# Reordering the projection prepass of a two-branch attention kernel, and the weight loads around it

## The chip, the cores and the metric

The kernel runs on one core of one Trainium2 chip. The metric is the device time of one execution in microseconds (us), taken as the median of several runs. Lower is better.

## The reference, cut to what matters

Two attention branches over the same 2048 tokens of 640 features are mixed by a gate.

```python
def _A_ref(x, mem0, Wq, Wk, Wv, Wo, seg_len):      # H=32 heads of Dh=192, M=8 memory rows, seg_len=32
    mem = mem0
    for s in range(n_seg):                           # 64 segments, one after the other
        h = concat([mem, x[:, s*32:(s+1)*32]], axis=1)      # 40 rows
        q, k, v = h @ Wq, h @ Wk, h @ Wv             # 640 -> 32 heads x 192, each
        p = softmax(where(mask, q k^T * scale, -1e9))
        o = (p v) @ Wo
        mem = o[:, :8]                               # carried to the next segment
        outs.append(o[:, 8:])

def _B_ref(x, wqkv, wo):   # 32 heads of 20; each query sees 8 keys at distance 0, 2, ..., 14
    ...

g = sigmoid((x * gate_w).sum(-1, keepdims=True))
return g * _A_ref(...) + (1 - g) * _B_ref(x, B_wqkv, B_wo)
```

Branch A is a recurrence: segment s+1 needs the first eight output rows of segment s.

## The kernel before, in words

**Order of the work.** The program runs four stages. `part_b` computes branch B and stores its gated result (`bsc_dram`), and on the way it stores the transposed inputs that branch A needs: `xh_dram` (one block of 40 columns a segment) and `zT_dram` (of each segment the last eight rows, 512 columns in all). `prepass` computes ahead of the recurrence the Q, K and V projections of those 512 columns, and stores them by segment in `zpk_dram`. `part_a` is the recurrence of 64 segments. `part_z` at its end makes the output rows that the recurrence leaves out.

**The weights of branch A.** Wq, Wk, Wv and Wo are cut into 80 slices of 128 partitions x 1536 bf16 (384 KB each, 3 KB of a partition): `("q", R, kc)`, `("k", R, kc)` and `("v", R, kc)` for four groups of heads R and five blocks kc of 128 input features, twelve `("oa", i)` and eight `("ob", i)` of Wo. Fourteen (`stream_keys`, N_STREAM) don't stay in SBUF: they are loaded again for every use into the five buffers of `wstream` (tile `wst`). The other 66 stay. Before, eleven of these are loaded early, in part B (`load_early`, tiles `wres_...`; q slices), and 55 late (tiles `wlate_...`) in three parts: 33 after part B into the room that it leaves, 21 after the Q/K projections of the prepass, and one after the prepass. The slices of Wo that are streamed (three) are first copied, early, from DRAM to a scratch tensor in DRAM (`wscr`), in which each partition's 3 KB lie in one piece; in `A_Wo` itself they are pieces of 768 or 512 bytes.

**The prepass.** `zT` holds the 512 columns, and `zTi` the same ordered by row within the segment (copied by GpSimd). First q, then k, each in two rounds `Rp` of two groups R: 24 outputs of 128 x 512 a round, five matmuls each (L424), which ACT and DVE in turn (`evac`, L71 and L73) copy from PSUM into a staging tile `ZS` (24 KB of a partition, two buffers). A round ends with one store of 3 MB on ACT's queue (L429), in pieces of 384 bytes. Then come the four V rounds: each has four tiles of 128 columns, three PSUM banks a tile (L438), copied into `ZV` (3 KB, two buffers), and each tile is stored by two DMAs of 192 KB on ACT's queue (L445), in pieces of 768 bytes. PSUM has eight banks, used in turn as `ps_pre`.

**Queues.** All weight loads are issued on SP's queue (`nc.sync`). On the same queue are, in part B, the stores of `xh_dram` (L182) and `zT_dram` (L187), from single-buffered tiles that GpSimd fills, and the loads of the gate. ACT's queue (`nc.scalar`) has the loads of x, the stores of `bsc_dram`, the load of `zT`, all stores of the prepass and all small loads of the recurrence (`hT`, `ZQ`, the last columns of `hT` from the initial memory in `A_mem`). An engine issues in its program order, so a DMA that has to wait holds up what stands behind it on that engine. Outside the recurrence the order of each engine's instructions, and the semaphores, are made by the builder from the data dependences, its own estimates of time and the order of the text; `tc.issue_after(first_store)` keeps the early loads and the prepass behind the first store of part B. In the recurrence PE, ACT and DVE follow an order written by hand. SBUF is full to within a few KB of a partition: pools that are closed make room for later ones, and a tile in such a place waits for what lay there (`reuse_waits="tile"`: tile by tile).

Of the kernel before, what the change touches and what calls it, by code (L numbers as in the profile page):

```python
# [10 lines left out]
BF = mybir.dt.bfloat16  # L11
F32 = mybir.dt.float32
I32 = mybir.dt.int32

N_STREAM = 14
N_LATE = 55
N_LATE2 = 22
WBUFS = 5

_DEV = {"mode": "full"}  # L20
# [4 lines left out]
class _K:  # L25
# [313 lines left out]
    def weights_setup(self):  # L339
        nc, tc = self.nc, self.tc  # L340
        keys = self.slice_keys()
        gap = {("q", 0, 0): 300, ("k", 0, 1): 160, ("k", 0, 3): 70, ("k", 1, 0): 450, ("k", 2, 0): 850, ("k", 3, 0): 1050,
               ("v", 1, 0): 1000, ("v", 2, 0): 600, ("v", 3, 0): 570, ("v", 3, 3): 200, ("oa", 6): 1200}
        at, t = {}, 0
        for k in keys:
            t += gap.get(k, 0)
            at[k] = t
            t += 163
        self.stream_keys = set()
        for i in range(N_STREAM):  # L350
            left = [k for k in keys if k not in self.stream_keys]
            self.stream_keys.add(min(left, key=lambda k: abs(at[k] - (i + 0.5) * t / N_STREAM)))
        rest = [k for k in keys if k not in self.stream_keys]
        first = ["q", "k", "v", "oa", "ob"]
        self.late = sorted(rest, key=lambda k: first.index(k[0]))[-N_LATE:]
        self.wres = self.ctx.enter_context(tc.tile_pool(name="wres", bufs=1))
        self.res_tiles = {}
        self.wscr = {}
        self.early = [k for k in rest if k not in self.late]
        self.wstream = self.ctx.enter_context(tc.tile_pool(name="wstream", bufs=WBUFS))  # L360

    def load_early(self):

        for k in self.early:
            self.res_tiles[k] = self.load_slice(self.wres, k, "wres_" + "_".join(map(str, k)))
        so = sorted(k for k in self.stream_keys if k[0] in ("oa", "ob"))
        scr = self.dram.tile([len(so), 128, 1536], BF, name="wscr")
        for i, k in enumerate(so):
            src, split = self.slice_info(k)
            self.nc.sync.dma_start(scr[i].rearrange("p (c f) -> p c f", c=split[0]), src)  # L370
            self.wscr[k] = scr[i]
# [10 lines left out]
            self.nc.sync.dma_start(v[:], src)  # L382
        return v

    def load_late(self, part):

        pool = self.ctx.enter_context(self.tc.tile_pool(name=f"wlate{part}", bufs=1, reuse_waits="tile"))
        ks = (self.late[:-N_LATE2], self.late[-N_LATE2:-1], self.late[-1:])[part]
        first = ks[:4] if part == 1 else []
        place = [k for k in ks if k not in first] + first  # L390
        tiles = {k: pool.tile([128, 1536], BF, name="wlate_" + "_".join(map(str, k))) for k in place}
        for k in ks:
            self.res_tiles[k] = self.load_slice(None, k, None, t=tiles[k])

    def get_slice(self, key):
        if key in self.res_tiles:
            return self.res_tiles[key]
        return self.load_slice(self.wstream, key, "wst", "wst")

    def prepass(self):  # L400

        nc, tc, KC = self.nc, self.tc, self.KC
        nseg = self.S // self.seg
        NZ = nseg * 8
        self.zpk_dram = self.dram.tile([nseg, 128, 1152], BF, name="zpk_dram")
        with tc.tile_pool(name="pre_zv", bufs=2, side="right", reuse_waits="tile") as zvp:
            zTi = zvp.tile([128, KC, NZ], BF, name="zTi", bufs=1)
            with tc.tile_pool(name="pre_zs", bufs=2, reuse_waits="tile") as zp, \
                    tc.tile_pool(name="pre_zt", bufs=1, reuse_waits="tile") as ztp:
                zT = ztp.tile([128, KC, NZ], BF, name="zT")  # L410
                nc.scalar.dma_start(zT[:], self.zT_dram[:].rearrange("p c s i -> p c (s i)"))
                nc.gpsimd.tensor_copy(zTi[:].rearrange("p c (i s) -> p c i s", i=8),
                                      zT[:].rearrange("p c (s i) -> p c i s", i=8))
                for m in ("q", "k"):
                    for Rp in range(2):
                        ZS = zp.tile([128, nseg, 192], BF, name="ZS")
                        for r in range(2):
                            sls = [self.get_slice((m, 2 * Rp + r, kc)) for kc in range(KC)]
                            for j in range(4):
                                for t in range(3):  # L420
                                    ps = self.pst([128, NZ], F32, name="ps_pre")
                                    c0 = 384 * j + 128 * t
                                    for kc in range(KC):
                                        nc.tensor.matmul(ps[:], lhsT=sls[kc][:, c0:c0 + 128], rhs=zT[:, kc, :],  # L424
                                                         start=(kc == 0), stop=(kc == KC - 1))
                                    zc = 96 * r + 8 * (4 * t + j)
                                    self.evac(ZS[:, :, zc:zc + 8], ps[:].rearrange("p (s i) -> p s i", i=8))
                        z0 = 768 + 192 * (1 - Rp) if m == "q" else 384 + 192 * Rp
                        nc.scalar.dma_start(self.zpk_dram[:, :, z0:z0 + 192].rearrange("s p f -> p s f"), ZS[:])  # L429
            self.load_late(1)  # L430
            for R in range(4):
                sls = [self.get_slice(("v", R, kc)) for kc in range(KC)]
                for st in range(NZ // 128):
                    ZV = zvp.tile([128, 1536], BF, name="ZV")
                    pss = [self.pst([128, 512], F32, name="ps_pre") for _ in range(3)]
                    for kc in range(KC):
                        for g in range(3):
                            nc.tensor.matmul(pss[g][:], lhsT=zTi[:, kc, 128 * st:128 * st + 128],  # L438
                                             rhs=sls[kc][:, 512 * g:512 * g + 512], start=(kc == 0),
                                             stop=(kc == KC - 1))  # L440
                    for g in range(3):
                        self.evac(ZV[:, 512 * g:512 * g + 512], pss[g][:])
                    for k in range(2 * st, 2 * st + 2):
                        dst = self.zpk_dram[:, 8 * R + k:128:32, 0:384]
                        nc.scalar.dma_start(dst, ZV[64 * (k % 2):64 * (k % 2) + 64, :].rearrange(  # L445
                            "s (j f) -> s j f", j=4))

    def build_sel(self, pool, ones):
        nc = self.nc
# [469 lines left out]
```

## Time and profile before

| | |
|---|---|
| three timed runs | 1772.72, 1776.31 and 1780.4 us; median 1776.31 |
| span of the profiled execution | 1775.1 us (the page has no other time of this execution) |
| PE busy | 1674.0 us (94%) |
| ACT, DVE, POOL busy | 870.1 (49%), 651.2 (37%), 72.7 us (4%) |
| DMA | 461.12 MB, mean 260 GB/s; SP's queue 395.75 MB, ACT's 60.12 MB |
| granted TensorE clock, mean | 0.991 |

The stages, read off the timeline: part B to 225.6 us; the prepass's Q and K to 332.0, its V to 397.4; the recurrence from 408.1 to about 1712, some 20.4 us a segment; then `part_z`. PE is busy when a matmul is in its pipeline, so 94% is not 94% of its peak. A line number is that of the code above; L71 and L73 are `evac`'s, L382 the load in `load_slice`, L370 the copy to scratch.

### The profile page before, as it was taken

Reading aid. Unit: us, or ns where it says so; the run is one execution under the profiler, and the core shown is the slowest. Engines: PE = TensorE matmul, PEld = TensorE weight load, DVE = VectorE, ACT = ScalarE, POOL = GpSimd, SP = SyncE. Lnnn points to the kernel's source line nnn. Section 1 sums busy time; section 2 is a strip of 40 time slices with the busy share of each in tenths; the row PEclk is TensorE's granted clock in tenths of the full one; section 3 lists DMA queues with packets and bytes.
Section 4 is the critical chain, followed back from the end, with each engine's and each line's share of the span. In section 5 each row is a group of like instructions: output and inputs, shape, how many; then the busy total and the mean of one; then the engine's idle time right before and its main releaser. Section 6 shows DMA issues by size and latency. Waiting matters only on the chain.

```text
span 1775.1 us, 82404 instructions
## 1 busy us (share of the span) xinstructions
PE 1674.0 (94%) x36512; PEld 997.3 (56%) x36527; DVE 651.2 (37%) x2047; ACT 870.1 (49%) x2377; POOL 72.7 (4%) x151
## 2 busy tenths in 40 slices
PE   6998999887999999999999999999999999999989
PEld 3554644334565655555556555555555556555557
DVE  4556533222333333333333333333333333333320
ACT  3766622223555555555555555555545555545550
POOL 4001000002000000000000000000000000000000
PEclk9999999998999999999999999999999999999999
DMA  6610195798899999999999999999999999989981
GB/s 164 203 32 29 46 315 171 207 283 233 293 301 307 305 300 301 300 299 304 300 294 304 308 293 308 298 297 297 305 292 299 301 297 304 303 289 300 299 282 30
DMA packets 280968, 461.12 MB, mean 260 GB/s; under 512 B 97188, under 2 KB 158116, under 8 KB 280612
## 3 DMA queue, kind: packets, MB, share of 16 engines
q1 hardware_dynamic: 173464, 395.75, 67.5%
q10 hardware_dynamic: 107148, 60.12, 11.9%
q8 instruction: 285, 4.67, 1.0%
q14 instruction: 71, 0.58, 0.1%
HBM read 421.44 MB, written 35.52 MB: 257 GB/s over the span
## 4 chain that ended last, share of the span: by engine, by line
PE 84%; ACT 6%; DMA 4%; issue 3%; DVE 2%; ACTq 1%; DVEq 0%
PE ps_qk L540 25%; PE ps_v L633 13%; PE ps_wo L697 11%; PE ps_qkT L557 6%; PE ps_pre L424 6%; PE ps_S L587 5%; PE ps_oT L656 3%; PE ps_z L851 3%; PE ps_bqk L220 3%; ACT bP L243 2%; DMA zpk_dram<-ZV 2%; ACT ZQ L778 2%; PE ps_mem L707 1%; PE ps_S L596 1%; PE ps_bv L207 1%
## 5 line engine op out<-in xcount | busy, mean ns | idle before, releaser
L549 ACT CAST KV<-ps_qk 128x384 bf16<-128x384 f32 x448 | 208.7, 480 | 340.2 <-PE ps_qk L540 196.5
L540 PEld LDWEIGHTS <-hT 128*32 128x32 bf16 x10240 | 247.7, 96 | 163.8 <-issue 21.0
L540 PE MATMUL ps_qk<-wlate_k,hT 128*32 128x384 bf16 x4352 | 270.0, 329 | 2.0 <-issue 2.0
L564 DVE COPY ZQ<-ps_qkT 128x384 bf16<-128x384 bf16 x256 | 91.6, 358 | 382.4 <-PE ps_qkT L557 216.8
L633 PE MATMUL ps_v<-wlate_v,hT 128*32 128x384 bf16 x4096 | 225.3, 330 | 0.0
L605 ACT ACTIVATE ZQ<-ps_S 32x224 bf16<-32x224 f32 x512 | 178.1, 348 | 43.7 <-PE ps_S L596 38.2
L697 PEld LDWEIGHTS <-KV 128*32 128x32 bf16 x6144 | 154.3, 96 | 67.0 <-issue 19.1
L540 PE MATMUL ps_qk<-wres_q,hT 128*32 128x384 bf16 x2816 | 164.2, 330 | 11.9 <-DMA hT<-in_A_mem_dram 10.7
L540 PE MATMUL ps_qk<-wst,hT 128*32 128x384 bf16 x1792 | 154.1, 328 | 0.6 <-DMA hT<-in_A_mem_dram 0.3
L633 PEld LDWEIGHTS <-hT 128*32 128x32 bf16 x5120 | 113.6, 96 | 66.8 <-issue 4.4
L697 PE MATMUL ps_wo<-wlate_oa,KV 128*32 128x384 bf16 x2560 | 140.4, 327 | 2.0 <-DVE ZQ L676 1.0
L587 PE MATMUL ps_S<-ZQ,KV 128*128 128x160 bf16 (+1 forms) x1024 | 136.9, 238 | 0.7 <-DMA ZQ<-zpk_dram 0.7
L697 PE MATMUL ps_wo<-wlate_ob,KV 128*32 128x256 bf16 x2688 | 124.2, 275 | 7.6 <-issue 7.5
L557 PE MATMUL ps_qkT<-ident,KV 128*128 128x128 bf16 x1536 | 130.0, 220 | 0.4 <-issue 0.4
L557 PEld LDWEIGHTS <-KV 128*128 128x128 bf16 x1536 | 89.0, 98 | 61.0 <-issue 40.8
L667 DVE CAST KV<-ps_oT 128x192 bf16<-128x192 f32 x256 | 79.2, 351 | 62.7 <-PE ps_oT L661 62.7
L587 PEld LDWEIGHTS <-KV 128*128 128x128 bf16 (+1 forms) x1024 | 58.8, 95 | 69.5 <-issue 42.2
L667 ACT CAST KV<-ps_oT 128x192 bf16<-128x192 f32 x256 | 69.6, 326 | 57.3 <-PE ps_oT L661 57.3
L710 DVE CAST hT<-ps_mem 128x24 bf16<-128x24 f32 x126 | 22.5, 179 | 199.1 <-PE ps_mem L707 199.1
L640 ACT CAST KV<-ps_v 128x384 bf16<-128x384 f32 x192 | 92.4, 481 | 3.3 <-PE ps_v L633 0.2
L633 PE MATMUL ps_v<-wst,hT 128*32 128x384 bf16 x1024 | 87.1, 330 | 2.4 <-DMA wst<-in_A_Wv_dram 2.4
L568 DVE COPY KV<-ps_qkT 128x384 bf16<-128x384 bf16 x256 | 89.0, 348 | 0.6 <-PE ps_qkT L557 0.4
(135 smaller groups left out, 2262.7 us busy)
## 6 DMA issues: line engine op xcount, KB each, us to landing
wst<-in_A_Wq_dram SPq DMA_DIRECT2D x260, 384.0 KB
wst<-in_A_Wv_dram SPq DMA_DIRECT2D x260, 384.0 KB
wst<-in_A_Wk_dram SPq DMA_DIRECT2D x195, 384.0 KB
wst<-wscr SPq DMA_DIRECT2D x192, 384.0 KB
zpk_dram<-ZS ACTq DMA_DIRECT2D x4, 3072.0 KB
ZQ<-zpk_dram ACTq DMA_DIRECT2D x64, 192.0 KB
wlate_k<-in_A_Wk_dram SPq DMA_DIRECT2D x17, 384.0 KB
wlate_v<-in_A_Wv_dram SPq DMA_DIRECT2D x16, 384.0 KB
```

Of the source, the lines that this page charges most:

```text
L424: nc.tensor.matmul(ps[:], lhsT=sls[kc][:, c0:c0 + 128], rhs=zT[:, kc, :], start=(kc == 0), stop=(kc == KC - 1))
L540: nc.tensor.matmul(pq[32 * j:32 * j + 32, 0:384], lhsT=hT[:, kc, :], rhs=sl[:, 384 * j:384 * j + 384], start=(kc == 0), stop=(kc == KC - 1 ...
L549: cp(sts[i], pqs[i][:, 0:384])
L557: nc.tensor.transpose(pT[:, t, :, :, :].rearrange("p j b i -> p (j b i)"), st[:, 128 * t:128 * t + 128], self.ident[:])
L564: nc.vector.tensor_copy(q_blocks(R)[:, 1:5, :, :].rearrange("p b c i -> p c b i"), pT.rearrange("p t j b i -> p (t j) b i"))
L568: nc.vector.tensor_copy(KV[:, 384 * (R % 2):384 * (R % 2) + 384], pT.rearrange("p t j b i -> p (t j b i)"))
L587: nc.tensor.matmul(grid(h, par)[:, :, 0:80].rearrange("p j (b r i) -> p j b r i", r=2, i=8)[:, :, :, r, :], lhsT=KT[k0:k1, 12 * r + c:12 * ...
L605: nc.scalar.activation(E[ps], pSs[h][ps, :, 112 * j:112 * j + 112], ACT.Exp, scale=scale_a)
L633: nc.tensor.matmul(pvs[R][32 * j:32 * j + 32, 0:384], lhsT=hT[:, kc, :], rhs=sl[:, 384 * j:384 * j + 384], start=(kc == 0), stop=(kc == KC ...
L640: cp(V[R], pvs[R][:, 0:384])
L667: cps[j % 2](oTxs[2 * h + j // 2][:, 6 * (j % 2):6 * (j % 2) + 6, :], pos[j][:, 0:240].rearrange("p (c q) -> p c q", q=40)[:, :, 8:40])
L697: nc.tensor.matmul(pso[part][32 * jj:32 * jj + 32, 0:n], lhsT=oTxs[2 * (R // 2) + j // 2][:, 6 * (j % 2) + 3 * (R % 2) + t, :], rhs=o_weig ...
```

## The change

The V rounds of the prepass move: after each Q/K round (four: two of q, two of k) comes one V round. `ZS` is now one buffer in each of two pools used in turn, `zs0` and `zs1`; `zT` moves into the pool of `zTi` and `ZV` at the right end of SBUF. The store of a `ZS` is split into two DMAs (segments 0 to 7, and the rest). The 66 slices that stay are sorted by their first use in the prepass (`use`) and divided anew: 25 early; late part 0 with 22 after part B; part 1 with 8 before the last Q/K round's matmuls, in the place of `zs0`; part 2 with 11 after the prepass. So of Wo two thirds come in the last part. All Wo slices that are not early (twenty, not three) are copied to the scratch in DRAM, and are loaded from there. At the end of the prepass up to WBUFS stream slices that the first segment uses (here two, `("q", 0, 2)` and `("q", 1, 0)`) are asked for ahead (`self.ahead`). The same values are computed, by the same matmuls.

```diff
-N_LATE = 55
-N_LATE2 = 22
+N_EARLY = 25
+N_MID = 8
+N_LAST = 11
...
-        first = ["q", "k", "v", "oa", "ob"]
-        self.late = sorted(rest, key=lambda k: first.index(k[0]))[-N_LATE:]
+        use = [g for p in range(4) for g in (("qqkk"[p], 2 * (p % 2)), ("qqkk"[p], 2 * (p % 2) + 1), ("v", p))]
+        rest.sort(key=lambda k: use.index(k[:2]) if k[:2] in use else 99)
+        n = (0, N_EARLY, len(rest) - N_MID - N_LAST, len(rest) - N_LAST, len(rest))
+        self.early, *self.late = [rest[n[x]:n[x + 1]] for x in range(4)]
...
-        so = sorted(k for k in self.stream_keys if k[0] in ("oa", "ob"))
+        so = [k for k in self.slice_keys() if k[0] in ("oa", "ob") and k not in self.early]
...
-        ks = (self.late[:-N_LATE2], self.late[-N_LATE2:-1], self.late[-1:])[part]
+        ks = self.late[part]
...
     def get_slice(self, key):
         if key in self.res_tiles:
             return self.res_tiles[key]
+        if key in self.ahead:
+            return self.ahead.pop(key)
         return self.load_slice(self.wstream, key, "wst", "wst")
...
+        def project_qk(p, pool):
+            m, Rp = "qqkk"[p], p % 2
+            ZS = pool.tile([128, nseg, 192], BF, name="ZS")
+            sls = [[self.get_slice((m, 2 * Rp + r, kc)) for kc in range(KC)] for r in range(2)]
+            if p == 3:
+                self.load_late(1)
+            ...
+            for s0, s1 in ((0, 8), (8, nseg)):
+                nc.scalar.dma_start(self.zpk_dram[s0:s1, :, z0:z0 + 192].rearrange("s p f -> p s f"), ZS[:, s0:s1, :])
+
+        def project_v(R):
+            ...
+        with tc.tile_pool(name="pre_zv", bufs=2, side="right", reuse_waits="tile") as zvp, \
+                tc.tile_pool(name="pre_zs1", bufs=1, side="right", reuse_waits="tile") as zs1:
             zTi = zvp.tile([128, KC, NZ], BF, name="zTi", bufs=1)
+            zT = zvp.tile([128, KC, NZ], BF, name="zT", bufs=1)
+            ...
+            with tc.tile_pool(name="pre_zs0", bufs=1, reuse_waits="tile") as zs0:
+                project_qk(0, zs0)
+                project_v(0)
+                project_qk(1, zs1)
+                project_v(1)
+                project_qk(2, zs0)
+            project_v(2)
+            project_qk(3, zs1)
+            project_v(3)
+        first = [("q", 0, kc) for kc in range(KC)] + [("k", 0, kc) for kc in range(KC)] + [("q", 1, kc) for kc in range(KC)]
+        for k in [k for k in first if k in self.stream_keys][:WBUFS]:
+            self.ahead[k] = self.get_slice(k)
```

The bodies of `project_qk` and `project_v` that are left out are the loops of before.

More of the change, by code (lines that the diff above doesn't have):

```diff
@@ L358, in weights_setup @@
         self.wscr = {}
-        self.early = [k for k in rest if k not in self.late]
+        self.ahead = {}
         self.wstream = self.ctx.enter_context(tc.tile_pool(name="wstream", bufs=WBUFS))
@@ L383, in load_slice, with load_late @@
         return v
-    def load_late(self, part):
-        pool = self.ctx.enter_context(self.tc.tile_pool(name=f"wlate{part}", bufs=1, reuse_waits="tile"))
-        ks = (self.late[:-N_LATE2], self.late[-N_LATE2:-1], self.late[-1:])[part]
-        first = ks[:4] if part == 1 else []
-        place = [k for k in ks if k not in first] + first
-        tiles = {k: pool.tile([128, 1536], BF, name="wlate_" + "_".join(map(str, k))) for k in place}
+    def load_late(self, part, side=None):
+        pool = self.ctx.enter_context(self.tc.tile_pool(name=f"wlate{part}", bufs=1, reuse_waits="tile", side=side))
+        ks = self.late[part]
+        tiles = {k: pool.tile([128, 1536], BF, name="wlate_" + "_".join(map(str, k))) for k in ks}
         for k in ks:
@@ L405, in prepass @@
         self.zpk_dram = self.dram.tile([nseg, 128, 1152], BF, name="zpk_dram")
-        with tc.tile_pool(name="pre_zv", bufs=2, side="right", reuse_waits="tile") as zvp:
-            zTi = zvp.tile([128, KC, NZ], BF, name="zTi", bufs=1)
[L408 to L446, printed above, removed]
@@ new lines, in project_qk @@
+        def project_qk(p, pool):
[4 more added lines that the diff above has]
+                self.load_late(1)
+            for r in range(2):
+                for j in range(4):
+                    for t in range(3):
+                        ps = self.pst([128, NZ], F32, name="ps_pre")
+                        c0 = 384 * j + 128 * t
+                        for kc in range(KC):
+                            nc.tensor.matmul(ps[:], lhsT=sls[r][kc][:, c0:c0 + 128], rhs=zT[:, kc, :],
+                                             start=(kc == 0), stop=(kc == KC - 1))
+                        zc = 96 * r + 8 * (4 * t + j)
+                        self.evac(ZS[:, :, zc:zc + 8], ps[:].rearrange("p (s i) -> p s i", i=8))
+            z0 = 768 + 192 * (1 - Rp) if m == "q" else 384 + 192 * Rp
+            for s0, s1 in ((0, 8), (8, nseg)):
+                nc.scalar.dma_start(self.zpk_dram[s0:s1, :, z0:z0 + 192].rearrange("s p f -> p s f"), ZS[:, s0:s1, :])
@@ new lines, in project_v @@
+        def project_v(R):
+            sls = [self.get_slice(("v", R, kc)) for kc in range(KC)]
+            for st in range(NZ // 128):
+                ZV = zvp.tile([128, 1536], BF, name="ZV")
+                pss = [self.pst([128, 512], F32, name="ps_pre") for _ in range(3)]
+                for kc in range(KC):
+                    for g in range(3):
+                        nc.tensor.matmul(pss[g][:], lhsT=zTi[:, kc, 128 * st:128 * st + 128],
+                                         rhs=sls[kc][:, 512 * g:512 * g + 512], start=(kc == 0),
+                                         stop=(kc == KC - 1))
+                for g in range(3):
+                    self.evac(ZV[:, 512 * g:512 * g + 512], pss[g][:])
+                for k in range(2 * st, 2 * st + 2):
+                    dst = self.zpk_dram[:, 8 * R + k:128:32, 0:384]
+                    nc.scalar.dma_start(dst, ZV[64 * (k % 2):64 * (k % 2) + 64, :].rearrange("s (j f) -> s j f", j=4))
@@ new lines, in prepass @@
+        with tc.tile_pool(name="pre_zv", bufs=2, side="right", reuse_waits="tile") as zvp, \
+                tc.tile_pool(name="pre_zs1", bufs=1, side="right", reuse_waits="tile") as zs1:
+            zTi = zvp.tile([128, KC, NZ], BF, name="zTi", bufs=1)
+            zT = zvp.tile([128, KC, NZ], BF, name="zT", bufs=1)
+            nc.scalar.dma_start(zT[:], self.zT_dram[:].rearrange("p c s i -> p c (s i)"))
+            nc.gpsimd.tensor_copy(zTi[:].rearrange("p c (i s) -> p c i s", i=8),
+                                  zT[:].rearrange("p c (s i) -> p c i s", i=8))
+            with tc.tile_pool(name="pre_zs0", bufs=1, reuse_waits="tile") as zs0:
[7 more added lines that the diff above has]
+            project_v(3)
```

## The prediction, made before the result was known

> **What bounds the kernel now.** I read the page's slices first, then busy time by stage, then the chain of waits between 330 and 412 us, then the queues one by one. The page first:
>
> ```profile
> span 1775.1 us, 82404 instructions
> ...
> PE   6998999887999999999999999999999999999989
> ...
> DMA  6610195798899999999999999999999999989981
> GB/s 164 203 32 29 46 315 171 207 283 233 293 301 307 305 300 301 300 299 304 300 294 304 308 293 308 298 297 297 305 292 299 301 297 304 303 289 300 299 282 30
> ```
>
> One slice is 44.4 us. TensorE is full almost everywhere; its deepest hollow after the start is the eighth to the tenth slice, 311 to 444 us. DMA is nearly idle in the third to the fifth. Busy time by stage (columns: length, PE, PEld, DVE, ACT, POOL busy, granted clock, DMA share, GB/s), for the Q/K part of the prepass, the V part with what follows it, and the recurrence:
>
> ```profile
> 225.60:332.00 106.40, 103.53 (x471) 46.97 (x482) 32.50 (x47) 28.14 (x48) 0.00 (x0) 1.00 0.74 228
> 332.00:408.10 76.10, 54.18 (x236) 23.74 (x239) 17.39 (x32) 13.28 (x24) 4.05 (x20) 0.90 0.95 269
> 431.00:1711.00 1280.00, 1243.71 (x30912) 753.09 (x30915) 458.63 (x1694) 665.71 (x2007) 32.09 (x63) 1.00 0.92 301
> ```
>
> Q/K runs at matmul speed. The V part has 240 matmuls; at the steady 0.216 us from start to start they need 51.8 us, and they end at 397.4, after 65.4: **13.6 us of stall**. Then 10.7 us pass until the recurrence's first matmul (408.1). Together 24 us is all that this change can touch; the recurrence is full and the change leaves its instructions alone. The chain of waits there (start, us, what):
>
> ```profile
> 339.04 8.39 ACTq L445
> ...
> 347.47 3.17 DMA zpk_dram<-ZV
> ...
> 352.40 8.25 DMA zpk_dram<-ZV
> ...
> 398.97 3.85 DMA zpk_dram<-ZV
> ...
> 402.92 1.79 DMA hT<-xh_dram
> ...
> 405.84 3.52 DMA hT<-in_A_mem_dram
> ```
>
> ACT's first V store (L445) stands 8.4 us behind the Q/K store ZS issued at 332.96 on the same queue; later the two ZV buffers wait for their stores; the tail is the last V store, then hT, then mem0. TensorE's timeline shows where that bites, and the window beside it what a long stall does to the clock:
>
> ```profile
> 344.94 0.81 PE L438 MATMUL ps_pre<-wlate_v,zTi 128*128 128x512 bf16 x3
> 351.50 3.57 PE L438 MATMUL ps_pre<-wlate_v,zTi 128*128 128x512 bf16 x8 [5.75 <-DVE ZV L73]
> ```
> ```profile
> 348.00:350.00 2.00, 0.00 (x0) 0.00 (x0) 0.00 (x0) 0.00 (x0) 0.00 (x0) 0.56 1.14 305
> ```
>
> PE ran 13.7 us past the start of V on its eight PSUM banks before it stopped.
>
> **Part by part.** PE work: the same 480 + 240 matmuls, 106.4 + 51.8 = 158.2 us.
>
> *V rounds between Q/K pairs.* This removes the V stalls of rounds that stand in a row (13.6 us), and puts a ZS store (3.15 MB) ahead of every V round instead of one. Its undisturbed price:
>
> ```profile
> 306.12 0.37 ACTq L429 DMA_DIRECT2D zpk_dram<-ZS  x1
> ```
> ```profile
> 312.00:316.00 4.00, 3.95 (x20) 1.82 (x19) 1.21 (x2) 1.17 (x2) 0.00 (x0) 1.00 0.99 261
> ```
>
> 3.15 MB at 261 GB/s is 12.1 us. So for a round that starts at S: ZS is issued at S+1, ACT is let go at about S+12 (before: S+15.4, with some 1.6 MB of loads beside it, 4 us at the 400 GB/s of the load windows at 228 to 252), the first ZV store lands 3.2 later, a bank is free at S+16. PE stops at S+13 plus two or three banks of the next Q/K group, 1.08 us each: S+15.1 to S+16.2. Queued behind ACT's blocked store are the evacuations of the later tiles; PE waits for them. So the stall of a middle round is 0 to 1 us alone, 3 with a weight load beside it. Three rounds: 3 us (from -2.3, if the three 0.78 us waits of the Q/K groups go too, to 9). The split of ZS into two DMAs adds one 0.4 us issue each, hidden by the banks, 0.4 us a store if not.
>
> *The last V round* has nothing behind it. S+12 for ZS; the first pair of ZV stores, between 3.2 (alone) and 6.6 (mean of the chain's 8.25, 6.41, 5.79 and 5.74, beside loads), 5.4 taken, since late part 3 can start when ZS has landed; evacuation 1.1; the next pair 6.6, the last one 1.2 behind it: S+26.3. hT and mem0 as before, 5.3: S+31.6, while PE is done at S+13.0. Tail 18.6 against 10.7. Ends: all alone, 13.7; with 8.25 for each pair and 2 us of queue, 25.
>
> *zT moves to the right end of SBUF.* Before, its load was out of the way:
>
> ```profile
> 138.67 4.83 POOL L412 COPY zTi<-zT 128x2560 bf16<-128x2560 bf16 x1 [10.85 <-DMA zT<-zT_dram]
> ```
>
> Issued at 133.2, landed at 138.7. Fourteen more early slices push part B's pools up by 43 KB a partition; summed from the tile sizes in the code, its last pool (P and 1/Z tiles) then lies where zT, zTi and ZV go. P is read until about 223.5 us, so zT would land near 229 where PE wants it at 225.6: +3.4; with nothing overlapping 0, with loads beside it 6. I take 3. The zTi copy (4.8 us) has until 252.
>
> On the clock: the row above fell to 0.56 some 3 us into an idle stretch of 5.75, the 1.95 us stall at 360 did not lower it. The Trainium skill (TensorE: Matmul & The Clock Gate, Part 1) has the clock halved after an idle window of about 3.4 us and back after as long a busy one; the trace agrees, and by it a zT wait of 3.4 us would cost up to 2 us more.
>
> *25 slices early, 20 Wo copies to scratch, on SP ahead of the stores of part B:*
>
> ```profile
> 29.23 17.84 SPq L382 DMA_DIRECT2D wres_q<-in_A_Wq_dram  x11
> 47.12 4.27 SPq L370 DMA_DIRECT2D wscr<-in_A_Wo_dram  x3
> 51.49 2.79 SPq L182 DMA_DIRECT2D xh_dram<-xh_blk  x1
> 54.38 3.71 SPq L187 DMA_DIRECT2D zT_dram<-zx_blk  x1
> ```
>
> In the DMA windows a load of 393 KB takes 1.15 us there, a copy about 1.6. SP pauses until 41.4 for ACT's x loads, as now; then 23 x 1.15 + 20 x 1.6 = 58.5: the queue is free at 100. Block 1's xh store goes out then, not at 51. xh_blk has one buffer, so POOL's copy of block 2 (80.0) waits to about 103; POOL's next work is at 114.3 and 124.2, zT's last store at 127.9. Nothing on the path: 0, and 20 us if ACT is drawn in (a rival). In return 14 loads leave the prepass, which is no longer short of DMA, so that is worth nothing by itself.
>
> *Late weights in three parts.* Part 1 (22 loads, 22 us at 400 GB/s) is needed from 305 on: free. Part 2 (8) waits for the third ZS store, about 345, and is needed at 371: 10 us of loading, free; 10 if it slips behind. Part 3 (11 loads, 4.33 MB) replaces one load; the first needs it 18 us into the recurrence. At 300 GB/s it takes 14.4 and starts before the end of V: 1 us taken, 0 to 10. The two slices fetched ahead are the ones that SP fetched ahead already: 0.
>
> **Sum.** 225.6 + 3 + 158.2 + 3 + 18.6 = 408.4 against 408.1; with 1 for part 3 the span is 1776.4. The profiled execution gives no time but its span, 1775.1; the median is 1.2 above it. Forecast **1777.6 us**: the stalls go, and the same microseconds come back at both ends of the prepass. Own range 1768 to 1786. A difference under 0.5% (8.9 us) is about what a measurement of this kernel can't tell from none.
>
> **Rivals.**
>
> *A, it works: 1767.* zT is early enough and the last round's stores drain beside its own matmuls. For it: all traffic of the prepass (44.7 MB in the windows, 5.5 less now) fits in 158 us of matmuls at 260 GB/s. Against: the order on ACT's queue. Without zT's 3 and with a tail of 10.7, 1776.4 - 3 - 7.9 = 1765.5, and 1766.7 with the 1.2. Chance 0.20.
>
> *B, part B pays: 1791.* SP's 45 issues delay ACT. Semaphores tie the queues: SP's loads waited 9.8 us for an x load that they do not read. The other way round, ACT's x loads at 79.0 or its stores from 76.7 on would wait for a weight load until up to 100, with the exp and the copies of part B behind them, and PE behind those. It decides if a DMA of ACT is numbered behind a copy that SP issues after 77. 0 to 21, 13 taken. Against: no such wait of ACT in the trace. Chance 0.22.
>
> *C, the last stores starve: 1787.* Part 3's eleven loads are issued ahead of the last ZV pairs. From rows: ZV pieces are 768 bytes, weight rows 3072; taken in turn, the store has a fifth of 350 GB/s, 1.57 MB takes 22 us from S+13, so hT comes at S+35 and not S+26: +9. The Trainium skill (DMA: Bandwidth & Descriptors, Queues, rings and completion order) has engines take the queues in turn, packet by packet; a pair's 8.25 beside loads against 3.2 fits, and no run here shows packets. Decides if ZS's landing frees part 3's room. Chance 0.12.
>
> That the V rounds aren't executed where the text puts them (the builder orders instructions by its own estimate) has the rest, priced as the forecast.
>
> **How the numbers follow.** Forecast 0.46, A 0.20, B 0.22, C 0.12. Faster: most of A, 0.16; slower: nearly all of B and C and a little of the forecast, 0.34; within: 0.50. Leaving out 0.1 on each side, of A below and B above, gives 1764 to 1797.
>
> **What would show it.** Right: TensorE's first L424 matmul at 227 to 230; V rounds in the timeline between the pairs with waits under 3 us; the last zpk_dram<-ZV landing some 13 us after the last prepass matmul; the first ps_qk near 408. Wrong: waits of ACT on a DMA between 75 and 100 (B); the first ps_qk before 400 (A) or after 415 (C).

## The result, and the profile after

| | before | after |
|---|---|---|
| median of 20 runs each, us | 1777.24 (1770.25 to 1784.99) | 1789.86 (1782.39 to 1794.82) |
| ratio, 95% interval | | 1.0067 [1.0053, 1.0082] |
| span of the profiled execution | 1775.1 | 1784.7 |

The changed kernel is slower by 0.67%, some 12 us. Its page, first two sections and the DMA lines:

```profile
span 1784.7 us, 82420 instructions
...
PE   6999999995999999999999999999999999999989
...
PEclk9999999996999999999999999999999999999999
DMA  6950174478999989989999998999999999999991
GB/s 178 336 155 17 42 270 127 126 221 256 307 300 308 305 289 308 301 288 300 300 303 299 307 301 296 308 300 299 306 301 296 303 292 298 302 305 296 303 304 30
```

The shallow hollow of the eighth to the tenth slice has become one deep hole in the tenth (402 to 446 us, PE at half, mean clock 0.69). The second and third slices carry the early weights, as meant. Busy time by stage (columns as in the prediction): the prepass up to its last matmul, what follows up to the recurrence's first matmul, the recurrence.

```profile
227.06:400.04 172.98, 162.36 (x705) 72.14 (x720) 46.59 (x69) 39.06 (x69) 4.73 (x1) 0.95 0.62 185
400.04:421.36 21.32, 0.00 (x0) 0.03 (x1) 2.83 (x10) 1.66 (x3) 6.76 (x34) 0.58 0.79 215
466.00:1700.00 1234.00, 1201.74 (x30013) 727.62 (x30013) 444.99 (x1643) 645.30 (x1947) 31.07 (x61) 1.00 0.91 301
```

The first stage took 171.8 us before and takes 173.0 now: taking V apart gained nothing. The second took 10.7 and takes 21.3. The chain of waits (start, us, what), one Q/K and V round after the other:

```profile
222.27 4.74 DMA zT<-zT_dram
...
227.89 13.19 PE ps_pre L422 x49
241.13 10.74 PE ps_pre L422 x49
...
262.87 5.41 ACTq L444
268.32 5.71 DMA zpk_dram<-ZV
...
274.89 5.71 PE ps_pre L422 x13
...
308.50 5.56 ACTq L444
314.10 5.26 DMA zpk_dram<-ZV
...
352.80 5.47 ACTq L444
358.31 4.01 DMA zpk_dram<-ZV
...
393.98 6.17 ACTq L444
400.18 4.44 DMA zpk_dram<-ZV
...
408.28 4.53 DMA zpk_dram<-ZV
412.95 5.31 DMA hT<-xh_dram
...
420.98 4.64 DMA hT<-in_A_mem_dram
```

What was there once (ACT's V store standing 8.4 us behind the ZS store) is now there four times, with 5.4 to 6.2 us each. L444 is the V store in `project_v`, L428 the ZS store, L422 and L437 the Q/K and V matmuls. TensorE's timeline has the waits that come of it (in brackets: the wait and what ended it), and ACT's timeline shows what ACT did in the first of them:

```profile
227.06 0.61 PE L422 MATMUL ps_pre<-zT,wres_q 128*128 128x512 bf16 x1 [3.65 <-DMA zT<-zT_dram]
...
274.89 1.86 PE L422 MATMUL ps_pre<-zT,wres_q 128*128 128x512 bf16 x4 [3.81 <-DVE ZV L74]
...
320.32 0.38 PE L422 MATMUL ps_pre<-zT,wres_k 128*128 128x512 bf16 x1 [3.60 <-DVE ZV L74]
...
421.36 1.13 PE L558 MATMUL ps_qk<-wres_q,hT 128*32 128x384 bf16 x8 [21.32 <-DMA hT<-in_A_mem_dram]
```
```profile
256.78 1.04 ACTq L428 DMA_DIRECT2D zpk_dram<-ZS  x2
258.82 1.07 ACT L72 CAST ZV<-ps_pre 128x512 bf16<-128x512 f32 x2 [3.30 <-PE ps_pre L437]
262.27 0.59 ACT L72 CAST ZV<-ps_pre 128x512 bf16<-128x512 f32 x1 [2.38 <-PE ps_pre L437]
262.35 9.55 ACTq L444 DMA_DIRECT2D zpk_dram<-ZV  x4
274.12 1.07 ACT L72 CAST ZV<-ps_pre 128x512 bf16<-128x512 f32 x2 [11.27 <-DMA zpk_dram<-ZV]
```

Issuing four V stores of 192 KB took ACT 9.55 us, and from 262.9 to 274.1 it emptied no PSUM bank. The third wait of this kind was 2.17 us, at 363.19; together the three are 9.6 us. The clock adds to it:

```profile
274.00:276.00 2.00, 1.11 (x3) 0.40 (x3) 1.61 (x3) 1.56 (x3) 0.00 (x0) 0.50 0.11 37
```

A steady matmul takes 0.2158 us (120 in 25.9 us, first experiment). The trace lacks 15 of the 720 records, so the slow ones are counted by their groups of five: the first 22 behind zT cost 2.9 us too much (7.60 us), the 14 from 274.89 on 2.8 (5.84 us), and the 35 from 320.32 on 1.7 (9.24 us). 155.4 for 720 matmuls, 9.6 of waits and 7.4 of slow clock are 172.4 of the 173.0.

The balance of the two profiled executions: start of the prepass +1.5, its matmuls +1.2, from there to the recurrence +10.6, first segment up to its `oz_dram` store +2.6, the 62 segments behind it -2.9, the rest -3.3: rounded, +9.7 for the 9.6 measured. The 62 segments take 1252.0 to 1264.7 us in the single profiled executions of the kernels below, whose recurrence is the same, so -2.9 is scatter; the last term is taken up again at the last experiment.

### The profile page after: what moved, and what is told of

It is laid out like the page before. It is cut to its first block, busy times and chain, and to the rows that moved or that the text cites. A ratio compares the mean times of both kernels' runs of the same rounds, so it can differ in the third digit from the quotient of the medians.

```text
span 1784.7 us, 82420 instructions
## 1 busy us (share of the span) xinstructions
PE 1674.1 (94%) x36512; PEld 995.3 (56%) x36527; DVE 647.2 (36%) x2047; ACT 869.2 (49%) x2377; POOL 72.8 (4%) x151
## 4 chain that ended last, share of the span: by engine, by line
PE 82%; ACT 6%; DMA 5%; issue 2%; ACTq 2%; DVE 2%; SPq 1%; DVEq 0%
PE ps_qk L558 25%; PE ps_v L651 12%; PE ps_wo L715 11%; PE ps_pre L422 6%; PE ps_qkT L575 6%; PE ps_S L605 5%; PE ps_bqk L221 3%; PE ps_oT L674 3%; PE ps_z L869 2%; ACT bP L244 2%; ACT ZQ L796 2%; PE ps_pre L437 1%; ACTq L444 1%; DMA zpk_dram<-ZV 1%; PE ps_mem L725 1%
## 5 line engine op out<-in xcount | busy, mean ns | idle before, releaser
L558 PE MATMUL ps_qk<-wlate_k,hT 128*32 128x384 bf16 x4096 | 258.7, 330 | 1.2 <-issue 1.2
L558 PE MATMUL ps_qk<-wres_q,hT 128*32 128x384 bf16 x4096 | 227.5, 329 | 24.4 <-DMA hT<-in_A_mem_dram 22.4
L651 PE MATMUL ps_v<-wlate_v,hT 128*32 128x384 bf16 x2048 | 117.8, 329 | 0.0
L651 PE MATMUL ps_v<-wres_v,hT 128*32 128x384 bf16 x2048 | 106.1, 327 | 0.0
L651 PE MATMUL ps_v<-wst,hT 128*32 128x384 bf16 x1024 | 86.7, 329 | 2.7 <-DMA wst<-in_A_Wv_dram 2.7
```

What stands on the lines that cost most here:

```text
L558: nc.tensor.matmul(pq[32 * j:32 * j + 32, 0:384], lhsT=hT[:, kc, :], rhs=sl[:, 384 * j:384 * j + 384], start=(kc == 0), stop=(kc == KC - 1 ...
L651: nc.tensor.matmul(pvs[R][32 * j:32 * j + 32, 0:384], lhsT=hT[:, kc, :], rhs=sl[:, 384 * j:384 * j + 384], start=(kc == 0), stop=(kc == KC ...
```

## The experiments

Two theories stood against each other. **Queue:** the 3 MB store ZS on ACT's own queue holds ACT, the V stores and the evacuations behind it; moving V between the Q/K rounds makes ACT meet it four times. **Traffic or order:** the stores and loads of the prepass are too much for the DMA engines near its end, or the last V round is simply in the wrong place, whichever queue issues them. Beside them stood the start of the first segment (hT and the memory rows), and the early loads and copies.

In the table, ratios are to the kernel before, run on the same chip in turn; not all experiments ran on the same chip, so rows are compared by their ratios and not by their medians. "Stage" is, in the profiled execution, the time from the first prepass matmul to the `oz_dram` store of the first segment: it holds all that the change can touch behind part B, in one execution each. "Wait" is TensorE's wait ahead of the recurrence's first matmul.

| kernel | median us | ratio, 95% interval | start of prepass | stage | wait |
|---|---|---|---|---|---|
| before | | 1 | 225.6 | 203.4 | 10.7 |
| after | 1789.86 | 1.0067 [1.0053, 1.0082] | 227.1 | 217.7 | 21.3 |
| e1_zs_on_sp | 1774.34 | 0.9983 [0.9967, 1.0000] | 227.4 | 201.6 | 16.6 |
| e2_v_last | 1777.65 | 1.0013 [0.9995, 1.0031] | 228.0 | 205.6 | 14.8 |
| e3_early_hT | 1785.51 | 1.0053 [1.0035, 1.0070] | 229.5 | 207.9 | 7.8 |
| e4_20_early | 1787.92 | 1.0065 [1.0038, 1.0091] | 232.6 | 210.2 | 20.6 |
| e5_3_copies | 1785.90 | 1.0076 [1.0062, 1.0090] | 226.7 | 215.5 | 21.0 |
| e6_before_early_hT | 1775.49 | 1.0019 [1.0006, 1.0033] | 229.0 | 201.9 | 1.0 |
| e7_sp_early | 1772.29 | 0.9994 [0.9978, 1.0009] | 232.1 | 199.6 | 6.0 |
| e8_before_zs_on_sp | 1769.61 | 0.9978 [0.9965, 0.9991] | 228.8 | 199.4 | 13.9 |
| e9_v_last_sp | 1770.41 | 0.9972 [0.9953, 0.9990] | 225.7 | 198.9 | 14.9 |
| e10_v_last_sp_early | 1770.22 | 0.9973 [0.9947, 0.9999] | 232.4 | 191.2 | 1.0 |
| e12_before_sp_copies | 1771.92 | 0.9993 [0.9973, 1.0012] | 227.2 | 198.4 | 13.4 |

**1. ZS on SP's queue.** The changed kernel, one word changed:

```diff
-                nc.scalar.dma_start(self.zpk_dram[s0:s1, :, z0:z0 + 192]..., ZS[:, s0:s1, :])
+                nc.sync.dma_start(self.zpk_dram[s0:s1, :, z0:z0 + 192]..., ZS[:, s0:s1, :])
```

> The changed kernel with one edit: the stores of ZS go out on SP's queue, not on ACT's, so no V store stands behind one. Theory 1 (the order on ACT's queue): ACT is no longer held for 5.4 us after each Q/K pair, a pair of V stores lands in 3 to 4 us, PE's waits of 3.8, 3.6 and 2.2 us and the slow clock after them go (about 14 us), the last V store lands some 17 us after the last V round's start and not 25.7: 15 to 22 us below the changed kernel, so about 1767 to 1775 where that one has 1790 and the kernel before 1777. Theory 2 (DMA bandwidth: 4.7 MB a V round and its ZS in 13 us is more than the queues move, whoever issues): waits of 2 us or more stay in each middle round, and the time stays within 6 us of the changed kernel.

Measured 0.9983 against 1.0067: the whole loss is gone. Its prepass and what follows, by stage, and the V part of its first round on ACT:

```profile
227.39:385.10 157.71, 157.38 (x720) 70.80 (x720) 46.61 (x70) 38.90 (x70) 4.75 (x1) 0.99 0.71 203
385.10:401.69 16.59, 0.04 (x1) 0.03 (x1) 2.54 (x10) 1.35 (x3) 4.72 (x23) 0.59 0.77 185
```
```profile
259.10 1.95 ACTq L444 DMA_DIRECT2D zpk_dram<-ZV  x2
261.45 0.59 ACT L72 CAST ZV<-ps_pre 128x512 bf16<-128x512 f32 x1 [2.38 <-PE ps_pre L437]
262.60 2.23 ACTq L444 DMA_DIRECT2D zpk_dram<-ZV  x2
267.80 1.07 ACT L72 CAST ZV<-ps_pre 128x512 bf16<-128x512 f32 x2 [5.76 <-DMA zpk_dram<-ZV]
```

The same V stores now take ACT 1.95 and 2.23 us. This round starts at 255.15; ACT is emptying banks again 12.7 us later, not 18.2 us as before (274.12 against a start at 255.97), and in 157.7 us TensorE stops once, for 0.33 us (at 351.53, behind a V store that took 9.76 us). The store itself moves as many bytes through the same DMA engines in less time, and the DMA share rises (0.71 against 0.62). So it is the queue and not the amount of traffic that stalled the middle rounds. The edit also puts SP's weight loads behind the ZS store; what that adds to the gain was not tried by itself. The Trainium skill (DMA: Bandwidth & Descriptors, Issuing engines are not separate DMA queues) says that issuing on several engines saves only their issue time, usually small beside the transfer. The first half agrees with the rows (what ACT saves is issue time, 4.18 us and not 9.55), the second doesn't here: 9.55 us is more than the 5.71 us in which the first V store then landed.

At the end the kernel before still has the shorter wait (10.7 us against 16.6): the last ZS and the V stores are landing until 395.7, and hT and the memory rows then stand beside part 3's loads (the last eleven, issued from 395.0 on; the prediction counts the late parts from 1, the code from 0).

```profile
373.41 19.51 DMA zpk_dram<-ZS
392.94 2.71 DMA zpk_dram<-ZV
395.75 2.48 DMA hT<-xh_dram
...
400.96 8.62 DMA hT<-in_A_mem_dram
```

**2. The four V rounds behind all Q/K rounds**, all else as in the changed kernel (ZS again on ACT's queue):

```diff
-                project_v(0)
...
-                project_v(1)
...
-            project_v(2)
...
-            project_v(3)
+            for R in range(4):
+                project_v(R)
```

> The changed kernel with the four V rounds again behind all four Q/K rounds, its loads and tiles as they are. Theory 1 (a ZS store ahead of each V round): only the first V round has one, so one wait of 3 to 6 us and not three, and the last V round's stores drain beside its matmuls: the last V store lands 5 to 6 us after the last prepass matmul and not 12.8. 8 to 12 us below the changed kernel: about 1778 to 1782. Theory 2 (it is the loads, not the order): within 4 us of the changed kernel.

Measured 1.0013, 0.5% below the changed kernel. One stall of 5.11 us is left (at 355.01, where the kernel before had its 5.75), and the wait ahead of the recurrence is 14.8 us. Undoing the order alone removes most of the loss; changing the queue alone (1) removes all of it. So the new order costs time only while ZS stands on ACT's queue. The queue costs a little in the old order too, as 8 and 9 show. The last V store landed 5.8 us after the last prepass matmul, as expected; hT (5.78 us) and the memory rows behind it make up the rest of the wait. The other parts of the change (early loads, copies, late parts) thereby cost at most 0.3% (the upper end of the interval).

**3. The first hT early.** In the changed kernel the first segment's block and the memory rows (five loads of 2 KB) are loaded ahead of the prepass, into a tile of their own:

```diff
+            self.hT0 = self.const.tile([128, KC, 32], BF, name="hT0")
+            nc.scalar.dma_start(self.hT0[:].rearrange("p c t -> p (c t)"), self.xh_dram[0])
+            for kc in range(KC):
+                nc.scalar.dma_start(self.hT0[:, kc, 0:8], self.mem0[:, kc * 128:(kc + 1) * 128]...)
...
-            hT = load_seg(0)
-            for kc in range(KC):
-                nc.scalar.dma_start(hT[:, kc, 0:8], ...)
+            hT = self.hT0
```

> The changed kernel with the first segment's hT (its block of xh_dram and the five small loads of the initial memory) loaded in a tile of its own at the start of the prepass, not after the last V store. Theory 1 (12.7 us of the tail are hT and the memory rows, slowed by part 3's weight loads): the recurrence's first matmul comes 8 to 12 us sooner, and its first copy out of PSUM waits for the last V store: 7 to 10 us below the changed kernel, about 1780 to 1783. Theory 2 (the wait only changes its name: part 3's weights, or the room of the tiles, are late too): less than 3 us.

Measured 1.0053, 0.14% below the changed kernel, some 2.5 us, which lies within the intervals and not in the 7 to 10 us of theory 1. The wait ahead of the first matmul fell from 21.3 to 7.8, but new waits took its place inside the first segment:

```profile
406.24 0.83 PE L562 MATMUL ps_qk<-wres_q,hT 128*32 128x384 bf16 x8 [7.83 <-ACT ZV L72]
...
420.44 0.28 PE L618 MATMUL ps_S<-ZQ,KTz 128*128 128x128 bf16 x2 [3.41 <-POOL KTz L538]
...
427.93 0.51 PE L655 MATMUL ps_v<-wst,hT 128*32 128x384 bf16 x4 [3.60 <-DMA wst<-in_A_Wv_dram]
```

**4. Twenty early slices and not 25** (`N_EARLY = 20`), so that part B's pools lie lower and zT's room is free in time:

> The changed kernel with 20 slices loaded early, not 25 (27 and not 22 in late part 0), so that part B's tiles end 15 KB lower and zT's place is free. Theory 1 (zT waits for part B's room): zT is loaded about 130 us in, PE's first prepass matmul follows part B at once, no 3.65 us wait and no slow clock after it: 4 to 5 us below the changed kernel, 1785. Theory 2 (the early share is what counts, or zT waits for something else): no change, or slower because the five slices delay the first V round.

zT is loaded at 137 us and its wait is gone (0.69 us is left, for ACT): zT did wait for part B's room. The time is not changed by an amount that the measurement could tell (1.0065, interval of some 4.7 us to each side). In the profiled execution the stage is 7.5 us shorter, but part B ended at 231.9 us and not at 223.4, with stretches at a lower granted clock (0.92 from 180 to 222 us). What zT's wait costs in time is therefore not shown.

**5. Three copies and not twenty:**

```diff
-        so = [k for k in self.slice_keys() if k[0] in ("oa", "ob") and k not in self.early]
+        so = sorted(k for k in self.stream_keys if k[0] in ("oa", "ob"))
```

> The changed kernel with three copies of Wo slices to scratch as before, not twenty; the other Wo slices are loaded from Wo itself in pieces of 768 and 512 bytes. Theory 1 (the 17 copies lie beside part B and nobody waits for them): part B as long as in the changed kernel within its scatter, GpSimd's 32 us wait for the xh store gone, the time the same within 4 us, or up to 3 us longer where part 3's loads in small pieces slow the tail. Theory 2 (rival B: SP's 45 issues slow part B through the queue or through DMA): 5 to 13 us faster than the changed kernel, 1777 to 1785.

Measured 1.0076 (changed kernel 1.0067), and the prepass starts at 226.7 us (227.1): the seventeen extra copies cost part B nothing that could be told. In the changed kernel they hold SP's queue to 93.5 us,

```profile
59.63 33.83 SPq L373 DMA_DIRECT2D wscr<-in_A_Wo_dram  x20
93.57 0.58 SPq L183 DMA_DIRECT2D xh_dram<-xh_blk  x1
```

and block 1's xh store goes out behind them, as predicted; GpSimd waits 32 us for it, and nobody for GpSimd. With three copies this wait is gone, and so is one of 1.9 us in which ACT waited for an x load (at 81.6) and TensorE 0.45 us for ACT.

**6. The kernel before, with the first hT early** (the edit of 3):

> The kernel before with the first segment's hT loaded in a tile of its own at the start of the prepass. The tail of 10.7 us holds 5.3 us of hT and memory rows: the first ps_qk comes 4 to 6 us sooner, its copy still waits for the last V store. 3 to 5 us below the kernel before, 1772 to 1774. If the next wait takes its place (weights, the room of KV): less than 1.5 us.

Measured 1.0019. Its first ps_qk has no wait left to speak of (1.0 us), and the time did not fall (the interval, 1.0006 to 1.0033, says a little longer): 4.25 us of wait now stand at the first segment's transposes (for ACT's KV) and 2.68 at its KTz.

**7. Both: ZS on SP and hT early, in the changed kernel** (1 and 3):

> The changed kernel with both edits: the ZS stores on SP's queue, and the first segment's hT loaded early. In the run with the first edit alone (1774) the first ps_qk came 16.6 us after the last prepass matmul, and PE waited 5 us more for memory rows behind part 3's weights. Theory 1: both go, 8 to 12 us below that run, about 1763 to 1767, faster than both kernels. Theory 2 (the tail turns into a wait for part 3's slices of Wo, or for KV's room): 2 to 5 us, 1769 to 1772.

Measured 0.9994, no better than e1. The sum of the two single gains is not there.

**8. The kernel before, with ZS on SP** (one word, as in 1, on line 429 of the kernel before):

> The kernel before with the ZS stores on SP's queue. Only the fourth of them stands ahead of V stores there. Theory 1 (queue): ACT's 8.6 us issue and PE's 5.75 us wait with the slow clock after it shrink to under 2 us, the other V waits (0.9 to 2 us each, beside part 1's loads) stay: 4 to 7 us below the kernel before, 1770 to 1773. If it is as fast as the changed kernel with the same edit (1774), the moved V rounds are worth nothing once the queue is right. Theory 2 (bandwidth: ZS, V stores and 21 loads share the 16 engines): no change within 2 us, since the loads behind ZS on SP's queue come later.

Measured 0.9978. The 5.75 us stall behind the one ZS that was in V's way is gone. ACT's issue of the first four V stores, in the kernel before (first line) and here:

```profile
338.81 10.64 ACTq L445 DMA_DIRECT2D zpk_dram<-ZV  x4
```
```profile
336.54 1.95 ACTq L445 DMA_DIRECT2D zpk_dram<-ZV  x2
...
340.04 2.39 ACTq L445 DMA_DIRECT2D zpk_dram<-ZV  x2
```

This kernel has the V rounds in a row, with waits of 0.62, 1.90, 1.69 and 2.86 us between them, and yet it is as fast as e1 (0.9983), which has one of 0.33: e1's prepass ends 8 us sooner after its start (157.7 us against 165.7), and pays 16.6, 2.8 and 2.2 us of waits at the start of the recurrence, against 13.9.

**9. V behind Q/K, with ZS on SP** (1 and 2 together):

> The changed kernel with its four V rounds behind all four Q/K rounds (as in e2_v_last) and the Q/K stores ZS issued on SP's queue instead of ACT's (as in e1_zs_on_sp). Queue theory: with ZS off ACT's queue the one V stall of 5.1 us that e2_v_last still had, and the slow clock behind it, go; the tail of about 15 us stays. So 5 to 7 us below e2_v_last, 1770 to 1772, ratio 0.997 to 0.998: the order of the V rounds is then worth nothing (e1_zs_on_sp 1774.3). Rival, loads and stores compete for the DMA engines whichever queue they stand in: within 2 us of e2_v_last, 1776 to 1779, with the stall of 5 us still there under another name.

Measured 0.9972 against e2's 1.0013. The stall of 5.11 us is gone; two short ones are left, and the wait ahead of the recurrence is unchanged at 14.9 us:

```profile
348.94 2.32 PE L437 MATMUL ps_pre<-wres_v,zTi 128*128 128x512 bf16 x10 [0.82 <-DVE ZV L74]
...
356.65 2.32 PE L437 MATMUL ps_pre<-wres_v,zTi 128*128 128x512 bf16 x10 [1.08 <-DVE ZV L74]
...
400.44 1.12 PE L556 MATMUL ps_qk<-wres_q,hT 128*32 128x384 bf16 x8 [14.92 <-DMA hT<-in_A_mem_dram]
```

With ZS on SP, then, V between the pairs (0.9983) and V at the end (0.9972) differ by less than their intervals: the reordering is worth nothing that these runs can tell once the queue is right. This kernel beats the kernel before and the changed one; e8 does so with one word, and the two can't be told apart.

**10. The same with hT early:**

> e9_v_last_sp with the first segment's hT and memory rows loaded before the prepass into a tile of their own. Theory of the queue alone: as in e6 and e7, the wait at the start of the recurrence moves to what comes next there (KV's room, the streamed weights), so within 2 us of e9_v_last_sp. Rival, the memory rows are what the start of the recurrence waits for: 5 us below e9_v_last_sp, 1765 to 1767.

Measured 0.9973, as e9. But this is no proof that the wait only moves. The stage from the first prepass matmul to the first segment's store is 7.7 us shorter than e9's (191.2 against 198.9), and the prepass starts 6.7 us later (232.4 against 225.7). ACT's queue instructions show part of why: the builder put the early loads into the middle of part B.

```profile
52.08 3.24 ACTq L454 DMA_DIRECT2D hT<-in_A_mem_dram  x1
...
57.77 0.38 ACTq L454 DMA_DIRECT2D hT<-in_A_mem_dram  x1
...
81.19 0.35 ACTq L284 DMA_DIRECT2D bsc_dram<-bo  x1
```

One of them held ACT for 3.24 us, and the first store of branch B's result left at 81.2 us, in e9 at 76.4. e7 has the same rows (3.49 us, 81.2). In e3 and e6 the shift is smaller (79.1 and 77.9, where the kernels without these loads lie between 74.9 and 78.0). So the early load seems to have two sides, 8 us won at the one end and some 5 lost at the other. The late start alone is no proof: e4, without these loads, starts its prepass at 232.6 us too. The same loads behind part B were not tried.

**11. Sixteen idle matmuls ahead of the prepass**, in the changed kernel, in the gap in which TensorE waits for zT; their result is not used:

```diff
+            warm = self.pst([128, 512], F32, name="ps_warm")
+            w0 = self.get_slice(("q", 0, 0))
+            for i in range(16):
+                nc.tensor.matmul(warm[:], lhsT=w0[:, 0:128], rhs=w0[:, 128:640], start=(i == 0), stop=(i == 15))
```

> The changed kernel with 16 extra matmuls (128x512, result unused) ahead of the first projection, where TensorE otherwise waits 3.65 us for zT. If the slow 49 matmuls behind that wait (13.19 us, granted clock 0.50) come from the idle stretch itself: 49 matmuls after zT in 10.6 to 11 us. Rival, they are slow because the loads beside them take the SBUF or the clock is lowered by something else: 13 us again. The gain of at most 2.5 us can't be seen in the time of a single run; only the timeline counts here.

The windows of this kernel where the changed kernel had 0.50:

```profile
229.00:231.00 2.00, 2.00 (x11) 0.87 (x9) 0.00 (x0) 0.00 (x0) 1.36 (x1) 1.00 0.79 254
231.00:233.00 2.00, 2.00 (x11) 0.90 (x10) 0.00 (x0) 0.58 (x1) 2.00 (x1) 1.00 1.02 404
```

The clock stays at 1.00 and five matmuls take 1.08 us from the first group on, with the same loads beside them (404 GB/s). So the idle stretch itself, and not the loads, slows the matmuls behind zT. The Trainium skill (TensorE: Matmul & The Clock Gate, Part 1) has this rule: the clock is halved after an idle window of about 3.4 us and comes back after a busy one. The run agrees in kind; as a threshold for the length of a wait the figure doesn't hold here (2.68 us were enough in e12, last section). The extra matmuls end only at 230.6 us, so the prepass starts 3.5 us later than in the changed kernel, and the time of this one run (1791.12) can't show 2.5 us.

**12. The kernel before, ZS on SP and twenty copies** (8, and the edit of 5 the other way round). It asks where the 3 us at the end come from: the stretch from the `oz_dram` store of the last but one segment to the end of the span is 86.0 to 86.7 us in the four kernels with three copies and 83.5 to 84.6 in the others.

> The kernel before with the Q/K stores ZS on SP's queue (as in e8_before_zs_on_sp) and all twenty late Wo slices copied to DRAM scratch instead of three. In the profiles so far the stretch from the end of the last but one segment to the end of the span is 83.5 to 84.6 us in the kernels with twenty copies and 86.0 to 86.7 us in those with three. If the copies themselves make that difference: 83.5 to 84.6 us here and a time 2 us below e8_before_zs_on_sp, 1767 to 1768, ratio 0.9967. Rival, the difference comes from the layout of the late weights or from the clock of single executions: 86.0 to 86.7 us and 1769 to 1770, ratio 0.9978. With a DMA near its limit ahead of the prepass the twenty copies could also cost up to 2 us there.

84.8 us at the end, and 0.9993 in time, no better than e8. The profile speaks rather for the copies, the time doesn't, and one profile a kernel decides nothing at a microsecond. This stays open. It also means that e8's gain is not shown again here: with the same word changed, this kernel is not clear of the kernel before.

## Why the prediction was right in part

1777.6 us was forecast, 1789.9 measured. The range of 1764 to 1797 holds it; the forecast's own range (to 1786) doesn't, and the likeliest class, no change, was wrong: 1.0067, with the lower end of its interval at 1.0053. The upper end of the range was set by rival B, whose cause was not there: that the range holds the time is in part luck. By the steps:

- **zT, 3 us:** right in kind, as 4 shows. TensorE waited 3.65 us, but part B's last matmul had ended early, so the first matmul came 1.5 us later than before and not 3. The up to 2 us for the slow clock, which the prediction named and didn't add, were there, 2.9 us by the rows, and experiment 11 shows the cause.
- **A middle round, 0 to 1 us alone, 3 for the three:** here the sum failed. The picture was right up to the stop: in the first round, which starts at S = 255.97, ACT is let go at S+12.3 (12 forecast) and TensorE stops at S+15.1 (15.1 to 16.2). Two things came behind it. First, the V store's 3.2 us was taken from a row where no load landed beside it; between the rounds it took 5.71, 5.26 and 4.01, so the banks came free at S+18.9 and not S+16: 3.81, 3.60 and 2.17 us of wait, 9.6 for 3. The prediction's own price "with a weight load beside it", 3 us a round, was the one to take, since SP issued weight loads in each of these stretches (at 268.95, 314.59 and 360.72); how much of the longer landing is due to them is not shown. Second, the slow clock was weighed for zT and not for these waits: 2.8 and 1.7 us more. So the three rounds cost 14.1 us, beyond the step's upper bound of 9. The prepass took 173.0 us from first to last matmul and not 161.2. These 11.8 us (11.1 more than forecast for the rounds and 2.9 for zT's slow clock, less some 2.3 for the three waits of 0.78 us, which are gone) are more than the 8.3 us by which the sum fell short of the span (1776.4 against 1784.7): the start of the prepass, the recurrence and the end gave some back.
- **The last round, 18.6 us (13.7 to 25):** right in kind and nearly in size, 21.3. The last V store landed at S+25.7 (26.3 forecast). hT and the memory rows took 8.6 from there and not 5.3, with part 3's loads beside them (hT 5.31 us where it was 1.79).
- **Copies and early slices, 0:** right, by 5 and by the rows of SP (free at 93.5, 100 forecast) and ACT: apart from the 1.9 us for an x load at 81.6, which is the mark of rival B at 1.9 us where B took 13, ACT waited for no DMA in part B from 40 us on. Rival B falls.
- **Late parts, 0, 0 and 1 us:** right for the first two; the first segment took 2.6 us more than before, 1.1 of them in a second wait for memory rows (at 425.67), with a mean clock of 0.80 where it was 0.88.
- **The recurrence, 0:** it and the end were 6 us shorter in this execution; half of that lies within the scatter of the segments, the last 3 us are open.
- **Rival A** falls in an instructive way. Neither of its conditions was met in the changed kernel: zT was late, and the last V store landed 12.8 us behind the last matmul. In e1 nearly all stalls in the middle are gone, zT is late by 2.8 us only, and it ran in 1774.3, 0.9983: not 1767. The stores of the last round still don't drain beside its own matmuls there; the shorter prepass leaves the last ZS, V and part 3 to be moved afterwards. **Rival C** gave nearly the right time, 1787, and its mark (first ps_qk after 415) was there, at 421.4, but by another way: of part 3's loads four were issued at 405.3, just ahead of the last two V pairs, and seven at 412.9, when these had landed. The last V store landed at S+25.7 and not S+35; what took longer beside the loads was hT, by 3.5 us, and the memory rows. That the time came near is luck: the rounds in the middle, of which C says nothing, gave most of it.

The prediction's reading that ACT's first V store stands 8.4 us behind the ZS store on the same queue held the answer already. It was used to price the new order and not to ask for the other queue, which gained where the order didn't (e8 and e9).

## What to carry to other kernels

Before work is reordered to fit around a stall, see on which queue the long store stands and what its issuing engine owes to others behind it: here one word, SP for ACT, gave 0.8% on the changed kernel (1.0067 to 0.9983) and 0.2% on the kernel before (0.9978; with twenty copies beside it 0.9993, which is not clear of none), while the reordering gave nothing that could be told. A wait of some three microseconds is to be counted with the slow clock that can follow it, here another 1.7 to 2.9 us. And a load that is moved ahead is to be looked for in the profile where the builder puts it: of the 8 us won at the recurrence some 5 seem to have been paid for in the middle of branch B.

## What the runs showed of the hardware that was not expected

- An engine that issues small DMAs behind a large store in small pieces on its own queue is held for long: four V stores took ACT 9.55 us behind 3.15 MB in 384-byte pieces, 4.2 us (1.95 and 2.23) with that store on the other queue, though both were in flight together. It was 10.64 us in the kernel before and 4.34 (1.95 and 2.39) in e8. Whether it is the size of the store or that of its pieces that holds the engine was not tried.
- Bytes are no measure for small pieces. The memory rows are 10 KB in all, loaded in pieces of 2 bytes; their last load of 2 KB took 3.52 us before, where the 40 KB of hT took 1.79, and 4.64 (after) and 8.62 us (e1) beside the loads of part 3.
- The length of a wait alone does not decide on the clock: behind 2.68 us in e12 (at 369.15) and 2.81 us in e1 (at 227.39) the clock was granted at 0.50, behind 3.50 us in e3 (at 275.85) and 2.70 us in e4 (at 276.48) at 1.00. The 2.17 us at 363.19 in the changed kernel left it at 1.00.
